# A 128-row bias matmul, and step B's loads issued by ScalarE

## The chip, the cores and the metric

The kernel runs on one core of a Trainium2 chip. The metric is the device time of one execution in microseconds (us). Three executions of the kernel before took 1357.65, 1356.60 and 1356.08 us; the median is 1356.6 us. Five engines work side by side, each through its own list of instructions in order: PE (matmuls; weight loads, PEld, are shown apart), DVE (VectorE), ACT (ScalarE), POOL (GpSimd) and SP (SyncE, which only issues DMAs here). Sixteen DMA engines move data for all of them.

## The reference

The input x has shape (4, 3008, 256): four batches. Cut to what matters:

```python
X = np.fft.rfft(x, axis=1)
Yr = Xr @ w_r - Xi @ w_i + b_r
Yi = Xr @ w_i + Xi @ w_r + b_i
Yr, Yi = shrink(Yr, 0.01), shrink(Yi, 0.01)     # sign(Y) * max(|Y| - 0.01, 0)
y = np.fft.irfft(Yr + 1j * Yi, n=3008, axis=1).reshape(12032, 256)
h = y @ moe_w_in                                # 256 -> 2048
g = np.maximum(h, 0) + moe_alpha * np.minimum(h, 0)
out = g @ moe_w_out                             # 2048 -> 256
```

All of it is float32.

## The kernel before, in words

A transform of length 3008 = 47 x 64 is done in two steps each way, as matmuls with tables: step A (length 47), step B (length 64), then the mixing step M with `w_r` and `w_i`, then steps C and D back. The two layers of the second part follow, tile by tile. The spectrum is worked on in 12 pairs of frequency slots (`NPAIR`), named q = 0 to 11.

The change lies in the first batch, b = 0, which runs alone at the start, while later batches are woven into the second part. Its steps B, M and C form a software pipeline: the loop `for t in range(NPAIR + 1)` near the end. In turn t, PE does in this order `b_mm(t)` (8 instructions of 128 columns into `ps_b`, L426), `m_mm(t - 1)` (first the bias matmul, L466, then 24 matmuls of 256 columns, L473, into `ps_m`) and `c_mm(t - 3)` (4 of 256 columns, L548, into `ps_c`). Between them stand the evictions: `b_evac` (ACT, L440) and `b_evac2` (DVE and POOL, L446 and L450), which split the result of step B into a rounded part `Xh` and a rest `Xl`; `m_evac` (ACT's `Yc`, L499, then DVE's `Y`, L500); `c_evac` (ACT's `zst`, L561, and the store of it to HBM, which ACT issues, L565). Every turn also runs a few operations of `pump`, which turns the weights of the second part into rounded part and rest (`conv`, L273 to L292, on ACT, DVE and POOL, from raw pieces `cw_s` that SP loads).

What step B reads was left in SBUF by step A (`a0_s`). `b_load(t + 3)` copies one pair of it into a tile `bt` by two DMAs of 128 KB, each from 4 partitions of 32 KB to 128 partitions of 1 KB. There are three such tiles, so the copy for pair t + 3 can start when `b_mm(t)` has read its own. For b = 0 POOL issues all of them: those of pairs 0 to 2 ahead of the loop, those of pairs 3 to 11 within it. For the later batches SP issues copies of the same shape from HBM.

The bias enters as a matmul of its own: `ones`, 4 rows x 128, is the stationary operand and `rows`, 4 rows x 512, the moving one (for b_r and b_i a rounded part and a rest each). It starts the accumulation of `ps_m`; the 24 products are added to it.

The order is written out by hand; each engine runs its own instructions in this order. DMAs that SP and ACT issue take one of eight completion semaphores in turn (`DMAHW0` to `DMAHW7` below), those of POOL one of eight others (`DMASW0` to `DMASW7`); an instruction that issues a DMA first waits until the DMA before it on the same semaphore has landed.

Of the kernel before, what the change touches and what calls it, by code (L numbers as in the profile page):

```python
# [10 lines left out]
F32R = mybir.dt.float32r  # L11
# [5 lines left out]
ALU = mybir.AluOpType  # L17
# [76 lines left out]
def fft_mix_moe(ctx, tc, x, w_r, w_i, b_r, b_i, w_in, w_out, alpha, la, rb, lc, rd, lf, cf, sel, out):  # L94
    nc = tc.nc
    B, S, C = x.shape
# [27 lines left out]
    const = ctx.enter_context(tc.tile_pool(name="const", bufs=1))  # L124
# [6 lines left out]
    V, G, A, PE = nc.vector, nc.gpsimd, nc.scalar, nc.tensor  # L131

    def f(t):
        return t.bitcast(F32)
# [32 lines left out]
    def half(h):  # L167
        t = const.tile([128, 2, FH * 2 * C], F32R, tag=f"half{h}", name=f"w{h}")
        wi_h[h] = t[:, 0].rearrange("p (w k f) -> p w k f", w=2, k=CT)
        wo_h[h] = t[:, 1].rearrange("p (m w f) -> p m w f", w=2, f=C)  # L170
# [5 lines left out]
    bias = [None]  # L176
# [6 lines left out]
    def first_bias():  # L183

        raw = work.tile([4, 2, C], F32, tag="Yt", name="bias_f", bufs=1)
        hi = work.tile([4, 2, C], F32R, tag="Yc", name="bias_h", bufs=1)
        pick = work.tile([4, 129], F32, tag="ot", name="sel", bufs=1)
        nc.gpsimd.dma_start(out=pick, in_=sel)
        for i, b in enumerate((b_r, b_i)):
            for k in range(2):  # L190
                nc.gpsimd.dma_start(out=raw[2 * i:2 * i + 2, k], in_=b.unsqueeze(0).to_broadcast([2, C]))
        rows = const.tile([4, 2, C], F32R, tag="bias", name="bias_p")
        ones = const.tile([4, 128], F32R, tag="wd", name="ones")
        bias[0] = ones, rows

        def parts():
            V.memset(lam_s, -LAM)
            V.tensor_copy(out=ones, in_=pick[:, 0:128])
            V.tensor_copy(out=hi, in_=raw)
            V.scalar_tensor_tensor(out=rows, in0=f(hi), scalar=pick[:, 128:129], in1=raw, op0=ALU.mult, op1=ALU.add)  # L200

        return parts

# [8 lines left out]
    def load_rb(n0, n1):  # L212
        nc.sync.dma_start(out=rb_s[:, n0:n1], in_=rb[:, n0:n1])

    def load_cf(n0, n1):
        nc.gpsimd.dma_start(out=cf_s[:, n0:n1], in_=cf[:, n0:n1])
# [93 lines left out]
    def pump(n):  # L310

        while n > 0:
            if not conv_ops:
                conv_fetch()
                second = conv_second(*conv_old.pop()) if conv_old else []
                first = conv_first(*conv_raw.pop(0)) if conv_raw else []
                first, second = ([(op,) for op in ops] for ops in (first, second))
                if first and second:
                    conv_ops.extend([second[0] + first[0], first[1], second[1], second[2] + second[3] + first[2]])
                else:  # L320
                    conv_ops.extend(first + second)
                if not conv_ops:
                    return
            for op in conv_ops.pop(0):
                op()
            n -= 1
# [12 lines left out]
    def a_load(b, g):  # L339

        if g == 0:
            ad[b] = dram.tile([NQ, R, C], F32, tag="ad", name=f"ad{b}")
        src = x[b].rearrange("(p r) c -> p r c", r=R)[:, 4 * g:4 * g + 4]
        if b == 0:
            ts = [x_s[:, 4 * g:4 * g + 4]]
        elif b == 1 and g in X1_TAGS:
            tags = X1_TAGS[g]
            ts = [work.tile([NP, 4 // len(tags), C], F32, tag=tag, name="xt", bufs={"Yl": None, "gh": 4}.get(tag, 1))
                  for tag in tags]
        else:  # L350
            ts = [work.tile([NP, 4, C], F32, tag="xt", name="xt")]
        if (b, g) == (0, 0):
            ts = [ts[0][:, 0:2], ts[0][:, 2:4]]
        n = 4 // len(ts)
        for i, t in enumerate(ts):

            for p in ((0, 80), (80, NP)):
                nc.sync.dma_start(out=t[slice(*p)], in_=src[slice(*p), n * i:n * i + n])
        xt[b, g] = ts
# [50 lines left out]
    def b_load(b, q):  # L410
        t = work.tile([128, 2, C], F32, tag="bt", name="bt", bufs=3)
        if b == 0:
            src = a0_s.rearrange("(w s q) g r c -> q w s (g r) c", w=4, s=2)[q]
        else:
            src = ad[b].rearrange("(w s q) r c -> q w s r c", w=4, s=2)[q]

        for k in range(2):
            (nc.gpsimd if b == 0 else nc.sync).dma_start(out=t[:, k], in_=src[:, k])
        bt[b, q] = t

    def b_mm(b, q):
# [560 lines left out]
    with tc.manual_schedule():  # L982
        nc.gpsimd.dma_start(out=lf_s, in_=lf)
        bias_parts = first_bias()
        nc.gpsimd.dma_start(out=la_s, in_=la)
        V.memset(idle, 0.0)
# [13 lines left out]
        for n, (b, g) in enumerate(seq):  # L1000
            a_mm(b, g)
            if n >= 1:
                a_evac(*seq[n - 1])
            if n == NG:
                for q in range(3):
                    b_load(0, q)
                split_mix()
                bias_parts()
# [6 lines left out]
        def run(fn, q, *args):  # L1015
            if 0 <= q < NPAIR:
                fn(0, q, *args)
# [9 lines left out]

        for t in range(NPAIR + 1):
            run(b_mm, t)
            run(b_load, t + 3)  # L1030
            run(c_evac, t - 4)
            run(b_evac, t)
            run(m_evac, t - 2)
            run(m_mm, t - 1, ps_h)
            run(b_evac2, t)
            run(c_mm, t - 3)
            if t < NPAIR:
                pump(PT[min(t, len(PT) - 1)])
            if t in (2, 5):
                load_rb(2 * t + 8, 2 * t + 14)  # L1040
            if t < 8 and t % 2 == 0:
                load_cf(3 * t, 3 * t + 6)
            if 5 <= t < 10:
                a_load(1, t - 3)
            if t == 10:
                half(1)
                conv_m[1] = FT
# [46 lines left out]
        for b in range(B):  # L1094
# [24 lines left out]
            for q in range(NPAIR if b + 1 < B else 0):  # L1119
                i = BO[b + 1] + BP * q  # L1120
                at(i - BL, b_load, b + 1, q)
                at(i, b_mm, b + 1, q)
                at(i, b_evac, b + 1, q)
                at(i, b_evac2, b + 1, q)
                at(i + MM, m_mm, b + 1, q)
                at(i + M2, m_mm2, b + 1, q, when=mid)
                for n, k in enumerate(MP):
                    at(i + k, m_part, b + 1, q, n, when=mid)
                at(i + MP[6], m_evac1, b + 1, q)
                at(i + CM, c_mm, b + 1, q)  # L1130
                at(i + CM, c_evac, b + 1, q)
# [60 lines left out]
        for k in range(len(spairs) + SLAG):  # L1192
# [9 lines left out]
            if k >= SLAG:  # L1202
                n, t = spairs[k - SLAG]
# [43 lines left out]
```

## Time and profile before

| | |
|---|---|
| median of three executions | 1356.6 us |
| profiled execution | 1356.09 us |
| its span, first to last instruction | 1354.3 us |
| PE busy | 1339.6 us (99%) |
| DVE busy | 1037.7 us (77%) |
| ACT busy | 759.2 us (56%) |
| POOL busy | 379.5 us (28%) |
| granted TensorE clock | full (2.4 GHz) in all 40 slices |

The rest of the 1356.09 us, 1.8 us, lies ahead of the first and behind the last instruction. The first batch's steps B, M and C take the stretch from about 31 to 91 us. POOL, with 28% over the whole span, is busy for 18.32 of the 20 us from 40 to 60 us, so that the shares of the whole span say little of this stretch. The DMA row of the page's slices shows 9 tenths in the first two slices, which reach to 68 us.

### The profile page before, as it was taken

How to read it: one execution, taken by the hardware profiler on the slowest of the kernel's cores; microseconds unless marked ns; L12 is line 12 of the kernel's file. 1: busy time of each engine (PE TensorE's matmuls, PEld its weight loads, DVE VectorE, ACT ScalarE, POOL GpSimd, SP SyncE). 2: the span in 40 equal slices, each digit the busy share in tenths (PEclk: the TensorE clock that was granted, in tenths of full speed). 3: DMA queues.
4: the chain of work that ended last, by engine and by line, in shares of the span. 5: the costliest groups of instructions: out<-in, count | busy, mean ns of one | idle time of the engine just before them, and what ended most of it. 6: DMA issues, size and time to landing. Idle time of an engine off the chain costs nothing.

```text
span 1354.3 us, 25104 instructions
## 1 busy us (share of the span) xinstructions
PE 1339.6 (99%) x9208; PEld 1252.3 (92%) x9208; DVE 1037.7 (77%) x1931; ACT 759.2 (56%) x1528; POOL 379.5 (28%) x403
## 2 busy tenths in 40 slices
PE   9999999999999999999999999999999999999998
PEld 5979989999999999999999999999999999999998
DVE  2766866777777777776768888888888888888885
ACT  3566645665566655545556555555565556555553
POOL 3854742221322232222212211122112111221222
PEclk9999999999999999999999999999999999999999
DMA  9964223342334312111110110111011101110001
GB/s 238 261 173 152 82 94 98 103 136 85 97 97 129 98 64 81 45 59 47 36 36 1 40 28 2 39 28 27 6 36 28 28 6 36 29 28 8 21 17 28
DMA packets 88119, 89.66 MB, mean 66 GB/s; under 512 B 42318, under 2 KB 70449, under 8 KB 87996
## 3 DMA queue, kind: packets, MB, share of 16 engines
q1 hardware_dynamic: 79428, 76.76, 19.9%
q0 software_dynamic: 5168, 8.02, 2.3%
q10 hardware_dynamic: 3399, 3.27, 0.8%
q8 instruction: 73, 1.20, 0.4%
q14 instruction: 51, 0.41, 0.1%
HBM read 50.49 MB, written 34.34 MB: 63 GB/s over the span
## 4 chain that ended last, share of the span: by engine, by line
PE 96%; DVE 1%; DMA 1%; issue 1%; ACT 1%; POOL 0%; ACTq 0%; DVEq 0%
PE ps_h L785 24%; PE ps_h L680 14%; PE ps_m L486 6%; PE ps_o L887 6%; PE ps_o L888 6%; PE ps_o L886 6%; PE ps_d L611 4%; PE ps_o L718 3%; PE ps_o L717 3%; PE ps_o L719 3%; PE ps_b L426 3%; PE ps_m L473 3%; PE ps_a L387 2%; PE o_last L719 2%; PE o_last L717 2%; PE o_last L718 2%
## 5 line engine op out<-in xcount | busy, mean ns | idle before, releaser
L785 PE MATMUL ps_h<-yh,w 128*128 128x512 f32 (+1 forms) x960 | 315.6, 390 | 0.0
L824 POOL TENSOR_TENSOR l<-t,h 128x512 fp32r<-128x512 f32 x98 | 127.0, 1296 | 496.6 <-ACT h L822 456.7
L785 PEld LDWEIGHTS ps_h<-yh,w 128*128 128x128 f32 x960 | 180.0, 188 | 33.2
L789 DVE SCALAR_TENSOR_TENSOR sq<-sq,beta_s,ps_h 128x512 f32<-128x512 f32 (+1 forms) x240 | 168.0, 733 | 55.0 <-ACT sq L788 54.2
L680 PE MATMUL ps_h<-yh,w 128*128 128x384 f32 (+1 forms) x704 | 206.2, 335 | 2.7 <-DVE q L687 2.7
L785 PE MATMUL ps_h<-yl,w 128*128 128x512 f32 (+1 forms) x480 | 186.3, 388 | 0.0
L691 ACT ACTIVATE gh<-q 128x384 fp32r<-128x384 f32 (+1 forms) x192 | 99.1, 516 | 148.6 <-DVE q L687 147.5
L687 DVE SCALAR_TENSOR_TENSOR q<-q,beta_s,ps_h 128x384 f32<-128x384 f32 (+1 forms) x192 | 115.5, 601 | 79.9 <-ACT q L686 78.1
L692 POOL TENSOR_TENSOR gl<-q,gh 128x384 fp32r<-128x384 f32 (+1 forms) x90 | 96.6, 1073 | 267.0 <-ACT gh L691 259.5
L804 ACT ACTIVATE dh<-sq 128x768 fp32r<-128x768 f32 x112 | 94.8, 846 | 118.0 <-DVE sq L789 72.8
L788 ACT ACTIVATE sq<-ps_h 128x512 f32<-128x512 f32 (+1 forms) x240 | 133.1, 586 | 27.5 <-PE ps_h L785 23.0
L680 PEld LDWEIGHTS ps_h<-yh,w 128*128 128x128 f32 x704 | 129.3, 189 | 5.7 <-DVE q L687 2.2
L822 ACT ACTIVATE h<-t 128x512 fp32r<-128x512 f32 x98 | 62.0, 633 | 104.5 <-DVE t L820 101.2
L680 PE MATMUL ps_h<-yl,w 128*128 128x384 f32 (+1 forms) x352 | 116.5, 331 | 0.0
L686 ACT ACTIVATE q<-ps_h 128x384 f32<-128x384 f32 (+1 forms) x192 | 91.4, 476 | 35.5 <-PE ps_h L680 34.2
L719 PE MATMUL ps_o<-w,gl 128*128 128x256 f32 x384 | 107.9, 281 | 1.7 <-POOL gl L692 1.7
L718 PE MATMUL ps_o<-w,gh 128*128 128x256 f32 x384 | 108.3, 282 | 0.0
L717 PE MATMUL ps_o<-w,gh 128*128 128x256 f32 x384 | 107.9, 281 | 0.0
L785 PEld LDWEIGHTS ps_h<-yl,w 128*128 128x128 f32 x480 | 90.5, 189 | 13.6
L819 DVE TENSOR_TENSOR dl<-sq,dh 128x768 fp32r<-128x768 f32 x98 | 93.4, 954 | 3.8 <-ACT dh L804 3.6
L888 PE MATMUL ps_o<-l,sw_a 128*128 128x256 f32 x294 | 82.0, 279 | 0.0
L886 PE MATMUL ps_o<-h,sw_a 128*128 128x256 f32 x294 | 81.9, 279 | 0.0
(211 smaller groups left out, 3625.6 us busy)
## 6 DMA issues: line engine op xcount, KB each, us to landing
zt<-zd SPq DMA_DIRECT2D x32, 384.0 KB
ad<-ast SPq DMA_DIRECT2D x48, 192.0 KB
bt<-ad SPq DMA_DIRECT2D x72, 128.0 KB
zd<-zst SPq DMA_DIRECT2D x36, 256.0 KB
xt<-in_x SPq DMA_DIRECT2D x21, 320.0 KB
out<-oT SPq DMA_DIRECT2D x152, 32.0 KB
cw_s<-in_moe_w_in SPq DMA_DIRECT2D x8, 512.0 KB
cw_s<-in_moe_w_out SPq DMA_DIRECT2D x8, 512.0 KB
```

The source lines that it names most:

```text
L680: PE.matmul(ps, wi_h[m // FH][:, w, ct, 128 * (m % FH):128 * (m % FH) + 128], a[:, ct, 0:n], start=(k == 0), stop=(k == 3 * CT - 1))
L687: V.scalar_tensor_tensor(out=q, in0=q, scalar=beta_s[:, m:m + 1], in1=ps, op0=ALU.mult, op1=ALU.add)
L691: A.activation(out=hi, in_=q, func=AF.Copy)
L717: PE.matmul(a, hi[:, t], w[:, 0], start=(i, k) in first, stop=False)
L718: PE.matmul(a, hi[:, t], w[:, 1], start=False, stop=False)
L719: PE.matmul(a, lo[:, t], w[:, 0], start=False, stop=(i, k) in last)
L785: PE.matmul(ps, wi_h[m // FH][:, w, ct, 128 * (m % FH):128 * (m % FH) + 128], a[:, ct, 0:w1], start=(k == 0), stop=(k == 3 * CT - 1))
L788: A.activation(out=q[:, j], in_=ps, func=AF.Relu, scale=-1.0)
L789: V.scalar_tensor_tensor(out=q[:, j], in0=q[:, j], scalar=beta_s[:, m:m + 1], in1=ps, op0=ALU.mult, op1=ALU.add)
L824: G.tensor_tensor(out=l24, in0=t24, in1=f(h24), op=ALU.subtract)
L886: PE.matmul(o, wh, gh, start=first, stop=False)
L888: PE.matmul(o, wh, gl, start=False, stop=last)
```

## The change

The tiles of the bias matmul become 128 rows high. DVE sets both to zero at the start, and the four rows are written into them as before. The loads of pairs 3 to 11 of the first batch are issued by ACT instead of POOL; those of pairs 0 to 2 stay with POOL. In the loop `b_load` is called behind `b_evac` instead of right behind `b_mm`. The later batches' loads stay on SP.

```diff
-        rows = const.tile([4, 2, C], F32R, tag="bias", name="bias_p")
-        ones = const.tile([4, 128], F32R, tag="wd", name="ones")
+        rows = const.tile([128, 2, C], F32R, tag="bias", name="bias_p")
+        ones = const.tile([128, 128], F32R, tag="wd", name="ones")
+        V.memset(f(rows), 0.0)
+        V.memset(f(ones), 0.0)
         bias[0] = ones, rows
 
         def parts():
             V.memset(lam_s, -LAM)
-            V.tensor_copy(out=ones, in_=pick[:, 0:128])
+            V.tensor_copy(out=ones[0:4], in_=pick[:, 0:128])
             V.tensor_copy(out=hi, in_=raw)
-            V.scalar_tensor_tensor(out=rows, in0=f(hi), scalar=pick[:, 128:129], in1=raw, op0=ALU.mult, op1=ALU.add)
+            V.scalar_tensor_tensor(out=rows[0:4], in0=f(hi), scalar=pick[:, 128:129], in1=raw, op0=ALU.mult, op1=ALU.add)
@@ b_load
         for k in range(2):
-            (nc.gpsimd if b == 0 else nc.sync).dma_start(out=t[:, k], in_=src[:, k])
+            (nc.sync if b else nc.gpsimd if q < 3 else nc.scalar).dma_start(out=t[:, k], in_=src[:, k])
@@ the loop over t
             run(b_mm, t)
-            run(b_load, t + 3)
             run(c_evac, t - 4)
             run(b_evac, t)
+            run(b_load, t + 3)
             run(m_evac, t - 2)
```

On ACT, in turn t = 6 of the loop, the kernel before has this order (each row is an instruction: its line, its kind, out<-in, and the semaphores it waits for):

```order
L561 ACTIVATE zst<-ps_c 128x512 [waits DMAHW5_49,PE_49]
L565 DMA zd_493<-zst 128x2x256 [waits Activation_49]
L440 ACTIVATE Xh<-ps_b 128x4x128 [waits PE_49,Pool_49]
L499 ACTIVATE Yc<-ps_m,lam_s 128x512 [waits DVE_49]
L273 ACTIVATE conv<-cw_s 128x512 [waits DMAHW6_49]
L282 ACTIVATE w_253<-conv 128x2x256 [waits DVE_49]
L283 ACTIVATE conv<-cw_s 128x512 [waits Pool_49]
```

and the changed kernel, in the same turn, this one (its line numbers are two higher):

```order
L563 ACTIVATE zst<-ps_c 128x512 [waits PE_49]
L567 DMA zd_495<-zst 128x2x256 [waits DMAHW7_49,Activation_49]
L442 ACTIVATE Xh<-ps_b 128x4x128 [waits PE_49,Pool_49]
L420 DMA bt<-a_83 128x1x256 [waits DMAHW4_49,DMAHW1_49]
L420 DMA bt<-a_83 128x1x256 [waits DMAHW3_49]
L501 ACTIVATE Yc<-ps_m,lam_s 128x512 [waits DVE_49]
L275 ACTIVATE conv<-cw_s 128x512 [waits DMAHW0_49]
L284 ACTIVATE w_255<-conv 128x2x256 [waits DVE_49]
L285 ACTIVATE conv<-cw_s 128x512 [waits Pool_49]
```

Two DMA issues, each with a wait of its own, now stand between `Xh` and `Yc`; all else keeps its place. On POOL the same turn reads, in the kernel before

```order
L418 DMA bt<-a_83 128x1x256 [waits DMASW5_49,DMASW6_49,DMASW4_49,PE_49]
L418 DMA bt<-a_83 128x1x256
L450 TENSOR_SCALAR Xh<-Xh 128x4x64 [waits Activation_49]
L450 TENSOR_SCALAR Xl<-Xl 128x4x64 [waits DVE_49]
L285 TENSOR_TENSOR conv<-conv 128x512 [waits DVE_49,Activation_49]
```

and in the changed kernel

```order
L452 TENSOR_SCALAR Xh<-Xh 128x4x64 [waits Activation_49]
L452 TENSOR_SCALAR Xl<-Xl 128x4x64 [waits DVE_49]
L287 TENSOR_TENSOR conv<-conv 128x512 [waits DVE_49,Activation_49]
```

Here the two issues, and their wait for PE, are gone. PE's own order is the same in both kernels.

## Rows read from the trace of the kernel before

**Rows 1.** The page's chain of waits, by engine, shares of the span

```profile
PE 96%; DVE 1%; DMA 1%; issue 1%; ACT 1%; POOL 0%; ACTq 0%; DVEq 0%
```

**Rows 2.** Chain of waits, 40 to 62 us (start us, us, what): one turn

```profile
44.93 0.89 PE ps_b L426 x8
45.83 0.43 PE ps_m L466
46.25 3.04 PE ps_m L473 x24
49.29 0.86 PE ps_c L548 x4
```

**Rows 3.** Timeline of PE, 45 to 47 us (start us, us, engine, line, op)

```profile
44.77 1.05 PE L426 MATMUL ps_b<-rb_s,bt 128*128 128x128 f32 x8
45.76 0.50 PE L466 MATMUL ps_m<-bias_p,ones 4*128 4x512 f32 x1
46.18 0.51 PE L473 MATMUL ps_m<-wr_s,Xh 128*128 128x256 f32 x2
...
46.65 0.40 PE L473 MATMUL ps_m<-wr_s,Xh 128*128 128x256 f32 x2
```

**Rows 4.** Groups, 31 to 92 us (busy us, mean ns | idle before <-releasers)

```profile
L473 PEld LDWEIGHTS ps_m<-wr_s,Xh 128*128 128x128 f32 x96 | 14.7, 189 | 3.0 <-issue 2.5 <-ACT conv L283 0.5
...
L466 PE MATMUL ps_m<-bias_p,ones 4*128 4x512 f32 x12 | 6.0, 497 | 0.0
```

**Rows 5.** Timeline of PE, 1000 to 1004 us: 512 columns on 128 rows

```profile
999.80 0.39 PE L785 MATMUL ps_h<-yh,w 128*128 128x512 f32 x1
1000.03 0.39 PE L785 MATMUL ps_h<-yl,w 128*128 128x512 f32 x1
```

**Rows 6.** Timeline of DVE, 0 to 9 us

```profile
7.29 0.69 DVE L402 COPY a<-ps_a 96x512 f32<-96x512 f32 x1 [6.35 <-PE ps_a L387]
```

**Rows 7.** Chain of waits, 74 to 92 us: the last pair's step B

```profile
81.53 0.89 PE ps_b L426 x8
```

**Rows 8.** Instructions on tile bt, 30 to 92 us (duration ns min/median/max, first and last start)

```profile
L418 POOL DMA_DIRECT2D bt<-a x18: 682/686/789, 30.9 to 68.2; - x18
...
DMA to landing us min/median/max: 4.9/7.3/10.3
```

**Rows 9.** Timeline of SP, 152 to 160 us

```profile
153.52 1.29 SPq L418 DMA_DIRECT2D bt<-ad  x2
```

**Rows 10.** Stretches: us, busy of PE, PEld, DVE, ACT, POOL, PEclk, DMA share, GB/s

```profile
20.00:24.00 4.00, 2.89 (x8) 0.86 (x7) 1.54 (x5) 2.50 (x5) 3.01 (x5) 1.00 1.05 369
31.00:78.00 47.00, 46.90 (x334) 42.47 (x334) 37.32 (x50) 25.75 (x46) 40.95 (x54) 1.00 1.00 247
158.00:161.00 3.00, 3.00 (x25) 3.00 (x24) 3.00 (x4) 1.38 (x3) 2.92 (x3) 1.00 0.28 90
```

**Rows 11.** DMA queues (packets, MB, share of 16 engines) and issues, 31 to 78 us

```profile
q1 hardware_dynamic: 5193, 5.90, 51.2%
q0 software_dynamic: 2971, 4.02, 36.5%
q10 hardware_dynamic: 1665, 1.61, 11.8%
...
xt<-in_x SPq DMA_DIRECT2D x2, 320.0 KB
xt<-in_x SPq DMA_DIRECT2D x4, 160.0 KB
```

**Rows 12.** Timeline of ACT, 50 to 62 us

```profile
56.53 0.60 ACT L440 ACTIVATE Xh<-ps_b 128x512 fp32r<-128x512 f32 x1 [0.50 <-PE ps_b L426]
...
59.66 0.63 ACT L282 ACTIVATE w<-conv 128x512 fp32r<-128x512 f32 x1 [1.39 <-DVE conv L288]
...
61.90 0.60 ACT L440 ACTIVATE Xh<-ps_b 128x512 fp32r<-128x512 f32 x1 [0.54 <-PE ps_b L426]
```

**Rows 13.** Who waited for whom, 31 to 91 us (us in total, times, longest)

```profile
ACT zst L561 <- PE ps_c L548: 10.1, 6, 2.5
```

## The prediction

> **What bounds the kernel now.** I read the page's chain of waits first: 96% of the span hangs on PE [rows 1], so what PE is spared counts, unless something else comes late in its place. The change touches one stretch, the first batch's loop over 12 pairs, so next I read the chain there. It runs through PE without a gap: 0.89 us of step B, 0.43 of the bias matmul, 3.04 of the 24 products, 0.86 of step C [rows 2], a turn of 5.22 us. The third view is the DMA: from 31 to 78 us its engines are counted as busy all the time (share 1.00), POOL for 40.95 of 47 us, ACT for 25.75 [rows 10]. A shorter turn on PE thus asks more of two resources that have little or nothing to spare.
>
> **The bias matmul.** The 4-row matmul starts at 45.76 and the next at 46.18, 0.42 us later [rows 3], for 512 columns. With 128 rows, 512 columns follow each other in 0.23 us (999.80 to 1000.03) [rows 5]. That is 0.19 to 0.20 us per pair for its own slot. Weight loads are caught as well: the one behind the bias matmul stands idle 3.0 us in all, 0.25 each in 12 pairs [rows 4], and the first two products take 0.51 us where two others take 0.40 [rows 3]: 0.11 us more, which I take to be that weight load, not hidden behind the 4-row matmul. Ahead of it the same seems to happen: eight matmuls of step B need 0.89 us in the chain [rows 2], 0.11 each, so the eighth starts at about 45.55, and the bias matmul follows 0.21 later instead of 0.11, another 0.10. Together 0.40 us per pair, 12 pairs [rows 4]: 4.8 us. Bounds: 12 x 0.20 = 2.4 us if only the slot shrinks, 4.9 us if all of it does; a loss is excluded, since the slot on 128 rows is in the trace. I take 4.8, because both weight-load terms are seen in the rows.
>
> The page TensorE: Matmul & The Clock Gate of the Trainium skill (section "Why this matters for your kernels") says that a single matmul on 32 rows takes the same time as one on 128; by it the saving would be nothing. The trace differs: 0.42 against 0.23 us.
>
> The two memsets stand at the start of DVE, which has 6.35 us of idle time there [rows 6]; I cost them at nothing. Were that cover gone, they would cost less than two of the 0.69 us copies next to them, 1.4 us.
>
> **The loads.** POOL loses 18 issues of 686 ns, 12.3 us [rows 8], and its wait for PE. ACT gains 18 issues. The nearest issue of that shape on a hardware queue is SP's copy for the later batches, 1.29 us for two [rows 9]. So ACT gets about 1.2 us per turn ahead of `Yc`, on top of 25.75 / 47 x 5.22 = 2.9 us of present work [rows 10], in a turn that PE would do in 4.82 us. `Yc` is needed only by DVE's `Y` and step C a turn later, and ACT waits 10.1 us for step C's matmuls in six of the turns [rows 13]. I let that slack hide the issues; a rival below takes it away.
>
> What isn't hidden so easily is who moves the data. From 158 to 161 us two copies of this shape from SP are under way; they move 90 GB/s at a DMA share of 0.28 of 16 engines [rows 10], that is on 4 to 5 engines and no faster for being two. I take it that a hardware queue puts these copies on the same four engines, each at about 22.5 GB/s, while POOL's go round. With all 16 busy, from 20 to 24 us, 369 GB/s give 23.1 GB/s for each [rows 10].
>
> The page DMA: Bandwidth & Descriptors of the Trainium skill (section "Why a DMA increments its semaphore by 16 and not by 1") has it so: the queues of SP and ACT use the lowest-numbered engines whose count divides both outer sizes, here 4 and 128, and GpSimd's queue moves on from one copy to the next. The share of 0.28 agrees; which engines they are no run here shows.
>
> So the four engines have this to do from 31 to 78 us: all queues moved 5.90 + 4.02 + 1.61 = 11.53 MB, 18 x 128 KB = 2.36 MB of it `bt` [rows 8, 11]. The other 9.17 MB spread over 16 engines are 0.573 MB for each; 2.36 MB on four are 0.590. Of the 1.163 MB, 0.082 are the loads of x for the second batch (2 x 320 KB and 4 x 160 KB [rows 11], over 16), which nobody needs before the loop ends. The eight semaphores of SP and ACT go round over both, so in the new order these loads wait for copies that ACT has issued. Time for it: the first of these loads is issued at 30.9 us [rows 8], the last pair's step B stands at 81.53 us [rows 7] and would come at 77.5 with ten pairs' saving of 0.40; with about 2.3 us for first packet and last landing (an estimate: the issue to landing is 4.9 us at the least [rows 8], about half of it transfer), 44.3 us are left.
> - At 23.1 to 24.5 GB/s (24.5 is what 98 GB/s on four engines would be, a tenth above the 90 of the row) and with x behind: 1.081 MB take 44.1 to 46.8 us. Late by 0 to 2.5 us.
> - With x in between: 1.163 MB, 47.5 to 50.3 us. Late by 3.2 to 6.0 us.
> - At the rates that the queues show now, in the crowded stretch (share x 16 x 47 us: 14.7 GB/s on q0, 15.3 on q1, 18.2 on q10 [rows 11]): 38 + 32 = 70 us. Late by 26 us.
>
> The last is the far end; I think it too high, because busy time in a crowd counts waiting. I take 1.5 us, in the middle of the first case, since the semaphores hold x back.
>
> **The sum.** 1356.09 us of the profiled execution - 4.8 + 1.5 = 1352.8. The median of the runs is 0.5 us above the profiled execution, so 1353.3 us. What follows the loop (step D, the second part) hangs on the loop's end and I let it shift as a whole.
>
> **Rivals.**
> 1. The four engines starve step B. The same copies at 20 GB/s instead of 23 take 1.081 / 20 = 54.1 us, 9.8 us late: -4.8 + 9.8 = 5.0 us slower, 1361.6 us. It decides from 22.0 GB/s downwards, where 1.081 MB take 44.3 + 4.8 us. For it: the share of 1.00 [rows 10] and 90 GB/s on four. Against it: 369 GB/s were moved with all engines busy, and SP's loads can slip. PE would then wait for `bt` before step B, late in the loop.
> 2. ACT becomes the bound. In the turn from 56.53 to 61.90 us it has 5.37 us from one `Xh` to the next, with a wait of 1.39 us for DVE, which itself stands behind `Y` and so behind `Yc` [rows 12]. With two issues of 1.2 us that turn becomes 6.6 us, 1.8 above 4.82. Two such turns unabsorbed cost 3.6 us: -4.8 + 1.5 + 3.6 = 0.3 us, 1356.9 us. A wait at the semaphores would come on top, since `Yc` and the conversions queue behind it. Against it: the slack of 10.1 us.
> 3. The change does not do what it says: the slow slot comes from going over from step B's operands to the bias's, not from the four rows. Then PE saves nothing, and the loads have 48 us, enough in the first case above: 1356.6 us. Against it: the late weight load behind the bias matmul, where the operands on both sides are of one kind.
>
> **Chances.** The forecast 0.47, with a range of its own from 1351.7 (nothing given back) to 1355. Rival 1: 0.25. Rival 2: 0.20. Rival 3: 0.08. The range that should hold 8 in 10 goes from 1351.3 to 1363: above it lies a part of rival 1 towards its 26 us. What can be told from no change is about 0.2%, 2.7 us: faster below 1353.9, slower above 1359.3. Of the forecast 0.39 of 0.47 falls below, of rival 2 0.04; of rival 1 0.19 falls above, of rival 2 0.03. So faster 0.43, same 0.35, slower 0.22.
>
> **What would show it.** Right: the bias matmul's next neighbour starts 0.23 us after it, the weight loads of the products lose their 3.0 us, a turn is near 4.8 us in the first half of the loop, and PE waits little for `bt`. Wrong: the slot stays at 0.42 us; or PE's wait for `bt` in the later turns adds up to over 4.8 us; or ACT's `zst` waits no more for PE, and PE waits for `Xh` or `Y` instead. The prediction fails as a whole if the loads land later than a turn allows from the first ones on.

## The result, and the profile after

The changed kernel takes 1365.43 us in the median (1364.06 to 1366.42, 5 runs) against 1356.6 us (1355.21 to 1357.65) for the kernel before: a ratio of 1.0063, 95% interval 1.0053 to 1.0074. It is 8.8 us slower where 3.3 us faster was forecast. The profiled execution took 1364.06 us, 7.97 us more than that of before.

The chain of waits of the changed kernel, by engine, has lost five points of PE, most of them to DMA and DVE [rows 1]:

```profile
PE 91%; DMA 4%; DVE 2%; ACT 1%; issue 1%; ACTq 0%; POOL 0%; SPq 0%; DVEq 0%
```

The same chain from 31 to 42 us (start us, us, what) shows an undisturbed turn near the loop's start. The bias matmul stands at 0.23 us and the 24 products at 2.84, where they had 0.43 and 3.04 [rows 2]: 0.40 us less in a pair. (Each piece of the chain is counted from the end of the one ahead of it.)

```profile
35.95 0.89 PE ps_b L428 x8
36.85 0.23 PE ps_m L468
37.08 2.84 PE ps_m L475 x24
```

Of the groups from 31 to 100 us, the weight load behind the bias matmul has 0.6 us of idle time left of 3.0, and the bias matmul itself now waits for DVE's `Y`, which it never did [rows 4]:

```profile
L475 PEld LDWEIGHTS ps_m<-wr_s,Xh 128*128 128x128 f32 x96 | 16.4, 198 | 0.6
...
L468 PE MATMUL ps_m<-bias_p,ones 128*128 128x512 f32 x12 | 6.1, 511 | 6.4 <-DVE Y L502 6.4
```

So the edit of the bias does what it was to do, and the loop is longer all the same. Where, the starts of the 12 bias matmuls tell (us, read from the traces; the experiments' rows are used below, and "freed semaphores" is the second run of that name, with the first `x` loads back on SP):

```
before            31.8 36.1 40.5 45.8 51.0 56.2 61.4 66.7 71.9 77.1 82.4 86.7
after             32.6 36.6 40.6 45.8 50.6 55.9 68.9 75.4 80.3 85.1 90.1 95.3
wide bias alone   33.2 37.6 41.6 46.4 51.2 56.0 60.9 65.9 70.7 75.6 80.5 85.9
" and zd on SP    32.5 36.8 40.8 45.6 50.4 55.3 60.1 65.1 70.0 74.8 79.6 83.5
freed semaphores  33.0 37.0 42.3 47.4 52.2 57.1 63.4 70.3 77.7 82.8 89.3 99.6
quarter on ACT    31.7 36.3 40.3 45.3 50.4 55.6 62.0 68.2 73.3 78.2 83.2 88.1
" behind Yc       32.0 36.0 40.0 44.8 49.6 54.5 59.3 64.3 70.6 75.7 80.6 85.7
```

From the first to the last they span 54.9 us before and 62.7 after. Eleven turns shorter by 0.40 would be 50.5, so 12.2 us were added: 8.2 in the turn from 55.9 to 68.9 (13.1 against 4.8), 1.7 in the next, some 2.3 in all others. Ahead of the loop and behind it the two differ by under 1 us.

ACT in that turn (timeline; in brackets the idle time before an instruction and what ended it): `zst` is done at 56.6, and its store is issued only at 62.87. Two loads of `bt` follow that take 2.94 us from the start of the first to the end of the second, which is held in its turn until 66.88, and `Yc`, for which DVE waits 8.7 us, comes at 67.47.

```profile
56.07 0.57 ACT L563 ACTIVATE zst<-ps_c 128x512 f32<-128x512 f32 x1
62.87 0.37 ACTq L567 DMA_DIRECT2D zd<-zst  x1
63.34 0.60 ACT L442 ACTIVATE Xh<-ps_b 128x512 fp32r<-128x512 f32 x1 [6.69 <-DMA bt<-a]
64.48 2.94 ACTq L420 DMA_DIRECT2D bt<-a  x2
67.47 0.69 ACT L501 ACTIVATE Yc<-ps_m,lam_s 128x512 f32<-128x512 f32 x1 [3.53 <-DMA xt<-in_x]
```

The store had to wait since the eight completion semaphores of SP's and ACT's queues go round over all their transfers in the order of the program. The eighth before this store was the second half of a `bt` load, issued at 47.02 and landed at 62.8, 15.8 us later. PE in the same stretch (timeline) wanted that very half, and then `Y`:

```profile
60.04 0.61 PE L428 MATMUL ps_b<-rb_s,bt 128*128 128x128 f32 x4
62.84 0.71 PE L428 MATMUL ps_b<-rb_s,bt 128*128 128x128 f32 x4 [2.19 <-DMA bt<-a]
68.94 0.79 PE L468 MATMUL ps_m<-bias_p,ones 128*128 128x512 f32 x1 [5.38 <-DVE Y L502]
```

That is 7.57 us of idle PE. It is paid a second time in the clock. In windows (us, busy of PE, PEld, DVE, ACT, POOL, PEclk, DMA share, GB/s) the granted clock falls to its lower level, 1.2 GHz, while PE stands idle, and it comes back at about 72.7, 3.8 us after PE has resumed:

```profile
66.00:68.00 2.00, 0.00 (x0) 0.00 (x0) 0.00 (x0) 0.53 (x1) 0.00 (x0) 0.50 0.26 89
70.00:72.00 2.00, 2.00 (x11) 2.00 (x11) 0.95 (x3) 1.68 (x3) 0.95 (x2) 0.50 0.12 40
72.00:74.00 2.00, 2.00 (x16) 1.97 (x15) 0.00 (x0) 0.96 (x2) 1.62 (x3) 0.84 0.69 122
74.00:76.00 2.00, 2.00 (x16) 1.88 (x15) 1.65 (x3) 1.43 (x3) 0.28 (x1) 1.00 1.03 375
```

Half of 3.8 us, 1.9, is what that costs by this count: about the 1.7 us that the next turn is too long.

From 31 to 78 us the DMA engines as a whole are less busy than before, a share of 0.68 against 1.00, and POOL 22.57 us against 40.95 [rows 10]:

```profile
31.00:78.00 47.00, 38.62 (x279) 36.67 (x280) 25.69 (x37) 19.89 (x35) 22.57 (x29) 0.93 0.68 205
```

Yet the loads land later. The 18 halves that ACT issues take 5.0 to 15.8 us from issue to landing, median 9.2, against 7.3 and at most 10.3 [rows 8]. How transfers end tells why (us, from the completion events; a transfer gives 16 signals, called parts here, and of ACT's halves only 4 wait for data):

```
kernel           transfer, issued by       issue   12th part  last part
wide bias alone  bt half, GpSimd           59.76     67.1       67.8
wide bias alone  zd store, ACT             62.22     71.6       72.0
after            weights, SP               50.48     54.6       58.0
after            zd store, ACT             52.30     57.4       64.5
half the pairs   bt half, GpSimd           58.89     61.7       68.1
half the pairs   zd store, ACT             55.19     59.9       70.9
```

In these rows of the changed kernel (and of one below in which ACT issues every second pair's loads) twelve parts land soon, and the last comes 3 to 11 us behind them, whichever queue the transfer went through. With all loads on GpSimd the sixteen end close together. Of all transfers with 16 such parts that were issued from 36 to 90 us, the 13th part is over 1 us behind the 12th in 16 of 24 in the changed kernel, but in 0 of 45 in the kernel before, 0 of 45 with the wide bias alone, and 0 of 57 in the run below with a quarter of the bytes on ACT. So there are four engines that are behind, and four is what ACT's copies use: in the window from 66 to 68 us above, where nearly all the packets are ACT's, the share of 0.26 is 4.2 engines of 16, and 89 GB/s are 22 for each of four. (The events do not say which engine a part is from; that it is the same four each time is the plain reading.)

### The profile page after: what moved, and what is told of

Its sections match the earlier page's. It is cut to its first block, busy times and chain, and to the rows that moved or that the text cites. A ratio compares the mean times of both kernels' runs of the same rounds, so it can differ in the third digit from the quotient of the medians.

```text
span 1362.3 us, 25093 instructions
## 1 busy us (share of the span) xinstructions
PE 1338.3 (98%) x9208; PEld 1253.0 (92%) x9208; DVE 1035.7 (76%) x1933; ACT 759.3 (56%) x1528; POOL 369.1 (27%) x385
## 4 chain that ended last, share of the span: by engine, by line
PE 91%; DMA 4%; DVE 2%; ACT 1%; issue 1%; ACTq 0%; POOL 0%; SPq 0%; DVEq 0%
PE ps_h L787 24%; PE ps_h L682 13%; PE ps_m L488 6%; PE ps_o L889 6%; PE ps_o L890 6%; PE ps_o L888 6%; PE ps_d L613 4%; PE ps_o L720 3%; PE ps_o L719 3%; PE ps_o L721 3%; PE ps_b L428 2%; DMA bt<-a 2%; PE ps_a L389 1%; PE o_last L721 1%; PE o_last L719 1%; PE o_last L720 1%
```

## The experiments

Two theories stood after the trace. T1: ACT's in-order queue, held by completion semaphores that come round too soon, keeps `Yc`, `Xh` and `zst` waiting. T2: four engines carry what sixteen did, and everything that has a part on them lands late, however it is issued. T3 is the price of the issues alone. All times are medians, ratios are to the kernel before.

**The bias alone.** The loads go back to GpSimd and to their old place:

```diff
-            (nc.sync if b else nc.gpsimd if q < 3 else nc.scalar).dma_start(out=t[:, k], in_=src[:, k])
+            (nc.gpsimd if b == 0 else nc.sync).dma_start(out=t[:, k], in_=src[:, k])
```

> The 128-row bias matmul alone, every load of step B issued by GpSimd at its old place. If the bias slot and the weight loads round it give back 0.40 us in each of 12 pairs, as both traces show it slot by slot, the time is 1356.6 - 4.8 = 1351.8 us (1350.8 to 1352.8). Rival: the loads' pace holds the pairs (DMA share 1.00 in that stretch of the kernel before), then TensorE's gain turns into a wait for `bt` and the time is 1355 to 1356.6.

1354.94 us, 0.9988 [0.9979, 0.9996]: 1.8 us of 4.8, between the two. TensorE has hardly a wait until 80 us, a turn is 4.85 us, and the loop is 2.2 us shorter in the profile (52.7), not 4.4; it also began 1.4 us later in that execution. The late turns lose it, the last alone 1.4 us (5.3 where 3.9 was due). ACT's timeline has one of the places, a `zd` store held until an `xt` load has landed:

```profile
75.97 0.58 ACT L563 ACTIVATE zst<-ps_c 128x512 f32<-128x512 f32 x1
78.13 0.37 ACTq L567 DMA_DIRECT2D zd<-zst  x1
78.59 0.60 ACT L442 ACTIVATE Xh<-ps_b 128x512 fp32r<-128x512 f32 x1 [2.04 <-DMA xt<-in_x]
```

**The loads alone.** The changed kernel with the 4-row bias of before.

> ScalarE issues the loads from the fourth pair on, at the changed kernel's place, and the bias matmul has its 4 rows. If the two edits simply add (the loads cost 13.4 us of waits, the bias gives 4.8), 1356.6 + 13.4 = 1370 us. If transfers set the pace of the pairs, TensorE's extra 0.40 us a pair lies in the waits and the time is that of the changed kernel, 1365 us; between the two, part of it.

1365.85 us, 1.0068 [1.0056, 1.0080]. The second forecast holds. Beside the late loads the bias is worth 0.4 us, which is within the intervals: the transfers set the pace, and what PE is spared turns into waiting.

**SyncE issues the loads.**

```diff
-            (nc.sync if b else nc.gpsimd if q < 3 else nc.scalar).dma_start(...)
+            (nc.gpsimd if b == 0 and q < 3 else nc.sync).dma_start(...)
```

> The same loads, the same two copies a pair and so the same four DMA engines, issued by SyncE instead of ScalarE; 128-row bias. Theory T1 (ScalarE, held at an issue, keeps `Yc`, `Xh` and `zst` waiting behind it): most of the 13.4 us of waits go, 1352 to 1357 us, and ScalarE has no wait over 3 us before `Yc` or `Xh`. Theory T2 (the copies land 10 to 14 us after they were issued, since four engines carry them, whoever issues): the waits stay, now before `ps_b` for `bt`, 1361 us or more; SyncE's own loads queue behind them. Theory T3 (ScalarE's 0.55 us per issue): 1352 us.

1366.86 us, 1.0078 [1.0066, 1.0090]: as T2 says in time, but not in the place. ACT is free of issues and still waits, for weights that SP issues in between and that now come late (waits from 31 to 100 us: us in total, times, longest):

```profile
ACT conv L275 <- DMA cw_s<-in_moe_w_in: 9.3, 2, 7.3
...
PE ps_m L468 <- DVE Y L502: 8.1, 7, 2.0
...
ACT conv L275 <- DMA cw_s<-in_moe_w_out: 6.7, 2, 5.5
```

The halves land 4.3 to 11.4 us after their issue. This run takes the issues off ACT without parting the theories, since SP's queue is in order too. It does show that the loss doesn't need ACT as the issuer.

**The stores off ACT.**

```diff
-            nc.scalar.dma_start(out=dst, in_=st)
+            nc.gpsimd.dma_start(out=dst, in_=st)
```

> The changed kernel, with the 12 stores of step C's results of the first batch (`zd`) issued by GpSimd instead of ScalarE. T1 in the form that a store, held by its completion semaphore, stops ScalarE (the 6.7 us before `Xh` at 63 us): 1357 to 1361 us. T1 by the loads' own semaphores, or T2: 1363 to 1367 us, with the waits behind the `bt` issues.

1367.28 us, 1.0085 [1.0070, 1.0100]. The hold only moves on to the next instruction of ACT that needs a semaphore, a load, with `Yc` behind it (ACT's timeline; some of the time may be GpSimd's, since the same move beside the wide bias alone costs 2.8 us, 1357.72 against 1354.94 below):

```profile
56.33 0.59 ACT L442 ACTIVATE Xh<-ps_b 128x512 fp32r<-128x512 f32 x1
62.69 1.16 ACTq L420 DMA_DIRECT2D bt<-a  x2
63.90 0.69 ACT L501 ACTIVATE Yc<-ps_m,lam_s 128x512 f32<-128x512 f32 x1 [6.98 <-DMA bt<-a]
```

**Half the pairs on ACT** (pairs 4, 6, 8, 10; the others on GpSimd).

> The changed kernel, but ScalarE issues only the loads of pairs 4, 6, 8 and 10; GpSimd those of the others. T2: the four engines get less than half of the extra load, landing falls below the lead of about two turns and most of the 13.4 us goes: 1353 to 1359 us. If each ScalarE-issued pair costs a wait of its own (a share of 4/9): 1358 to 1361 us.

1360.00 us, 1.0019 [1.0010, 1.0028]: about half the loss (5.1 of 10.5 us over the bias alone) for 8 of the 18 copies; it lies in the second forecast and 1.0 us above the first, too near to part them. Its trace gave the rows on the late four parts above.

**Sixteen engines, by SyncE.** Each half is cut by source row into four copies:

```diff
+            for k in range(2):
+                for w in range(4):
+                    nc.sync.dma_start(out=t[32 * w:32 * w + 32, k], in_=a0_s[24 * w + 12 * k + q:24 * w + 12 * k + q + 1].rearrange("p g r c -> p (g r) c"))
```

> SyncE issues the loads from the fourth pair on, as in the run where SyncE issued two copies a pair (1366.9 us), but each copy is cut into four by its source row: 8 copies of 32 KB a pair, each from one row of 32 pieces, so that each lands with 16 increments instead of 4. Same bytes, same 1 KB pieces; four times as many issues, and four times as many completion semaphores taken. T2 (four engines carry what sixteen could): loads land in 4 to 8 us instead of 9 to 15, SyncE's other loads no longer end with four late engines, and the time is 1352 to 1359 us. T1 (semaphores held and in-order issue are the cost): no better than 1367 us, or worse, since 8 copies hold all 8 semaphores.

1377.58 us, 1.0158 [1.0139, 1.0178]. T2's landings came true, 2.7 to 5.7 us, all 16 parts within some 2 us of each other; its time did not: that is the one that T1 named, 1367 us or worse. But it needs no semaphore to explain it. SP issues 72 copies of 0.59 us (group of that line from 31 to 100 us: ns min/median/max), 4.7 us of a turn, and the weights stand behind them (waits from 31 to 115 us):

```profile
L422 SPq DMA_DIRECT2D bt<-a x72: 502/589/1842, 32.3 to 95.8; - x72
ACT conv L275 <- DMA cw_s<-in_moe_w_in: 20.0, 4, 9.9
ACT conv L275 <- DMA cw_s<-in_moe_w_out: 16.7, 3, 9.3
```

**Half the bytes on SyncE**, once as four copies on 16 engines, once as one on four; GpSimd has the other half.

> 128-row bias. From the fourth pair on, GpSimd issues one half (128 KB) of each load and SyncE the other half, cut into four copies of one source row each, which land with 16 increments; `zd` stays on ScalarE. To be read against the next run, which differs only in that SyncE's half is one copy that lands with 4 increments. T2 (crowding of four engines): no landing ends with four late engines, copies land in 3 to 6 us, and this run is the faster of the two by 3 us or more: 1351 to 1356 us against 1358 to 1363. T1 (semaphores alone): four times as many copies hold four times as many semaphores, and this run is the slower one.

> As the run before, with SyncE's half of each load as one copy of four source rows (four engines). T2: half of the extra load on the four engines, as in the run where ScalarE took four of nine pairs (1360.0 us): 1358 to 1363 us, landings of 128 KB in 8 to 14 us. T1: faster than the run before, 1352 to 1356 us.

1362.29 us (1.0041 [1.0027, 1.0055]) and 1359.76 us (1.0027 [1.0017, 1.0038]). The order is T1's, though the intervals overlap; the second's time is T2's, and neither theory has both times. In the second SP's halves landed 4.6 to 12.2 us after issue, and four late parts show in 17 of 38 transfers; the first, with `zd` on SP as well,

> The first run of this call with `zd` stores issued by SyncE too, so that ScalarE issues nothing in the pairs. If a held store on ScalarE is what is left: 1350.5 to 1353 us, under the first. If SyncE's row of issues (4 copies, 1 store, weights and `xt` a pair) is too long: 1355 us or more.

took 1360.89 us, 1.0032 [1.0019, 1.0045], and there too ACT waited 12.2 + 9.1 us for weights behind SP's issues. On SP the theories can't be parted: by these waits its own issues hold the kernel up before the relief of the engines can show.

**The same issues, a quarter of the bytes.** ACT's 18 issues stay, with their semaphores in the same order, but each carries one source row of four; GpSimd issues the other three.

```diff
+                nc.scalar.dma_start(out=t[0:32, k], in_=a0_s[12 * k + q:12 * k + q + 1].rearrange("p g r c -> p (g r) c"))
+                nc.gpsimd.dma_start(out=t[32:128, k], in_=src[1:4, k])
```

> The changed kernel with the same 18 issues on ScalarE at the same places and with the same completion semaphores in the same order, but each ScalarE copy carries one source row of four (32 KB, landing with 16 increments); GpSimd issues the other three rows of each half (96 KB). T1 or T3 (the issues on ScalarE and the semaphores they take and wait for are the cost in themselves): 1361 to 1366 us, with ScalarE held for 5 us or more at one issue. T2 (holds are long only because 128 KB on four engines lands 9 to 16 us after its issue): landings of 3 to 8 us, no ScalarE wait over 3 us, 1353 to 1357 us.

1359.36 us, 1.0018 [1.0006, 1.0030]: 6.1 us of the changed kernel's 10.5 over the bias alone are gone. ACT's copies land in 3.2 to 9.0 us, the 6.7 us hold is gone, and the DMA share is back at 0.92. T1 and T3 had said 1361 to 1366, T2 1353 to 1357, so the time lies between; of T2's signs the landings came nearly (3 to 8 us was said). What is left seems to be ACT's waiting for its own issues ahead of `Yc` (waits of ACT, 31 to 93 us):

```profile
ACT Yc L505 <- issue: 5.9, 4, 2.7
ACT Yc L505 <- DVE conv L277: 2.3, 1, 2.3
```

**The same with the load's call behind the one for `Yc`.**

> The run in which ScalarE issues one row of four (1359.4 us), with the load's call moved behind the one that puts `Yc` on ScalarE. There ScalarE spent 1.2 to 2.7 us a turn on two issues with `Yc` behind them. If what was left over the kernel with the wide bias alone (4.4 us) is `Yc` kept waiting by issues: 1354.5 to 1357 us. If it is the loads' lateness: 1359 us or more.

1358.19 us, 1.0007 [0.9996, 1.0017]. The loop of the profile shrinks from 56.4 to 53.7 us; the medians differ by 1.2 us and their intervals overlap, and the profiled execution was the fastest of 12, 3.3 us below the median. The median lies between the two forecasts. That `Yc` behind the issues is the rest is likely, and not shown.

**Freed semaphores.** `zd` and the second batch's `x` loads on GpSimd, so that a load of ACT waits for a transfer three turns old.

> The changed kernel (loads from the fourth pair on by ScalarE, 128 KB on four engines each) with the `zd` stores and the second batch's `x` loads issued by GpSimd, so that a load of ScalarE waits for a transfer three turns old instead of about one and a third. T1 (semaphores taken again too soon hold ScalarE): landings still 8 to 15 us, but the 7 us holds go and the time is 1353 to 1358 us. T2 alone (the loads are too late for TensorE, however they are issued): 1361 us or more, with TensorE waiting at `ps_b` for `bt`.

1378.62 us, 1.0155 [1.0133, 1.0176]; the pairs began at 41.4 us, since the first `x` loads kept GpSimd. With these back on SP:

> As the run with freed semaphores, but the second batch's first two `x` loads stay on SyncE, since on GpSimd they put the start of the pairs off by 9 us (first bias matmul at 41.4 us). T1: ScalarE's loads wait for transfers that are three turns old and are hardly held; 1353 to 1358 us, the pairs from first to last bias matmul in 53 to 56 us. T2: landings of 9 to 17 us as in that run, and the pairs need 62 to 67 us as there; 1363 to 1368 us.

1367.26 us, 1.0073 [1.0058, 1.0089], the loop 66.6 us long. These are T2's numbers, but in part by luck. The last two turns alone take 16.9 us (82.7 to 99.6) against 10.2 in the changed kernel, and there PE waits for GpSimd, which now issues the stores and most `x` loads too and is busy for 17.73 of 18 us (the window in the columns of above, then PE's waits from 31 to 105 us):

```profile
82.00:100.00 18.00, 13.15 (x74) 11.85 (x74) 13.13 (x20) 7.81 (x14) 17.73 (x26) 0.81 0.61 191
...
PE ps_m L475 <- POOL Xh L452: 4.9, 2, 3.7
PE ps_b L428 <- DMA bt<-a: 3.4, 3, 2.0
```

So the time of this run doesn't part the theories; the turns ahead of that stretch can. From the first to the tenth bias matmul it is 42.4 us with the wide bias alone, 52.5 in the changed kernel, 49.7 here and 46.5 with a quarter on ACT (one execution each). Of 10.1 us lost there, freed semaphores give back 2.8, and three quarters of the bytes taken off the four engines 6.0.

The loads stay late here. Landings take 5.4 to 17.7 us; after one at 53.0 eleven more land up to 87.8 us, that is a pair in 6.3 us (34.8 / 11 x 2), where a turn of PE is 4.85. And a hold comes back without any semaphore to wait for. The second of two issues lasts 3.90 and 4.99 us, each time with five earlier halves on their way (ACT's timeline of the later one), and `Yc` is behind it:

```profile
70.22 0.54 ACTq L420 DMA_DIRECT2D bt<-a  x1
...
70.80 4.99 ACTq L420 DMA_DIRECT2D bt<-a  x1
75.83 0.69 ACT L501 ACTIVATE Yc<-ps_m,lam_s 128x512 f32<-128x512 f32 x1 [4.69 <-issue]
```

**The bias with the stores elsewhere**, since a held `zd` store ate some of its gain.

> The 128-row bias with all loads of step B on GpSimd (1354.9 us), and the first batch's 12 stores of `zd` issued by GpSimd too. In that run ScalarE waited 2.0 us before `Xh` behind a store held until an `xt` load had landed. Theory: this hold on ScalarE ate part of the bias's 4.8 us; then 1351 to 1353.5 us. Rival: GpSimd (busy 0.94 of 44 to 56 us there) becomes the bound with 12 issues of 0.7 us more: 1355 to 1359 us.

> As the run before, but SyncE issues the `zd` stores, which leaves GpSimd as it was. Theory (a held store on ScalarE ate the gain): 1351 to 1353.5 us. Rival: SyncE, waiting for `zst` in order, starts its weight and `xt` loads later: 1355 us or more.

> The kernel before (4-row bias, loads on GpSimd) with only the first batch's `zd` stores moved to SyncE. With the 128-row bias the same move gave 1354.1 us. If the move itself brings nothing while TensorE is never idle in the pairs: 1356 to 1357 us, and the bias is worth 2 to 3 us on top of it; if it brings the gain alone: 1354 to 1355 us.

On GpSimd 1357.72 us (1.0008 [0.9999, 1.0017]), the rival's time. POOL is busy 42.74 of 47 us from 31 to 78, but PE waits for it only 0.8 us there, so that POOL is the bound is likely and not shown. On SyncE 1354.14 us (0.9979 [0.9970, 0.9989]), between the two forecasts, the fastest version here and better than both kernels, with a loop of 51.0 us, 3.9 below that of before, in a profiled execution that was the fastest of 9 and 1.4 us below the median. The move alone, with 4 bias rows, gives 1356.30 us (0.9994 [0.9983, 1.0006]), nothing that can be told. So the wide bias is worth 2.2 us on that ground, by intervals that overlap at their ends; against the bias alone on ACT's stores the 0.8 us gained are within the intervals.

## Why the prediction was wrong

**What bounds the kernel.** Read rightly: PE's chain in the loop, with DMA and POOL near their limit.

**The bias.** The size of the step holds to the hundredth: in the chain, slot 0.43 to 0.23, products 3.04 to 2.84, 0.40 us a pair. So does the reading of the idle weight load. The shares of its three terms do not hold, and that they add up right is luck in part. By the starts of the matmuls, as the prediction read them, the stretch ahead of the bias matmul shrinks from 0.98 to 0.81 us (0.10 was forecast), its own slot from 0.43 to 0.32 (0.20; the sign of being right, a neighbour 0.23 us later, didn't come in starts), and the products from 2.96 to 2.84 (0.11). What failed is to book 12 x 0.40 in full as time. It was worth 1.8 us alone, 2.2 with the stores moved, and 0.4, within the intervals, beside the late loads. Rival 3 falls, since the slot shrank between the same neighbours.

The Trainium skill's rule that a single matmul on 32 rows costs what one on 128 does (TensorE: Matmul & The Clock Gate, "Why this matters for your kernels") does not agree with this trace, where it is 4 rows: 0.43 against 0.23 us in the chain, 0.32 by starts. No run here has 32 rows.

**The memsets.** Right: 0.48 and 0.17 us, with 5.30 us idle behind them (DVE's timeline):

```profile
0.92 0.48 DVE L194 MEMSET bias_p<- 128x512 f32 x1 [0.92 <-PEq L1229]
1.38 0.17 DVE L195 MEMSET ones<- 128x128 f32 x1
...
6.92 0.69 DVE L404 COPY a<-ps_a 96x512 f32<-96x512 f32 x1 [5.30 <-PE ps_a L389]
```

**ACT's issues.** Mostly 0.54 to 0.62 us each, 1.15 for two, as taken from SP's row (1.2); four of the 18 took 1.0 to 1.6. Their slack was taken for cover of the issue time alone. The hold at a semaphore, which rival 2 names and does not price, is the larger part: ACT is idle for 6.69 and 3.53 us in one turn, of which the two issues themselves are 1.1. The prediction's own sign of being wrong is what came: `zst` waits 0.5 us for PE instead of 10.1, and PE waits for `Y`, 6.4 us, and 2.8 for `bt`, 0.6 of it ahead of the loop (waits, 31 to 100 us):

```profile
PE ps_m L468 <- DVE Y L502: 6.4, 3, 5.4
...
PE ps_b L428 <- DMA bt<-a: 2.8, 2, 2.2
```

**The loads: the step that failed.** "Late by 0 to 2.5 us", of which 1.5 was taken, rests on four engines at 23.1 to 24.5 GB/s and on "x behind". The four engines were right, the rate and the order were not. Its own row of 158 to 161 us gives 22.5 GB/s for each of four, and its range began above that. From 31 to 68 us the changed kernel's queues moved this (DMA view of that stretch):

```profile
DMA packets 6722, 7.71 MB, mean 208 GB/s; under 512 B 2572, under 2 KB 4872, under 8 KB 6718
```

Twelve halves of `bt` had landed by 68.3, 1.57 MB; a sixteenth of the other 6.14 MB and a quarter of these make 0.777 MB on each of the four, 21.0 GB/s (an estimate: it takes the rest as spread evenly). And the `x` loads did not stay behind: four of the six pieces were issued between 52.9 and 72.8 us, before the last `bt` at 77.37. They are three quarters of the 0.082 MB, so the prediction's own sum is 1.081 + 0.062 = 1.143 MB; at 21.0 GB/s it takes 54.4 us, 10.1 late. With 1.9 for the clock, which the prediction put at nothing without a reason, -4.8 + 10.1 + 1.9 = 7.2 us stand against the 7.97 measured. So the term that was taken as 1.5 us came out as some 10: the case with x in between, at a rate just below the 22.0 from which rival 1 decides. That the new sum comes so near is luck in part. The last half lands at 88.0 us, where the sum has it at 30.9 + 2.3 + 54.4 = 87.6; but the four engines were not busy throughout (all engines have a share of 0.12 from 70 to 72 us, while ACT was behind with its issues), and PE did not wait for that half: it lost its time in the middle of the loop.

Rival 1 had the cause and the side. Its 1361.6 us has 20 GB/s where 21.0 came out, and leaves out the `x` loads (2.9 us at 21.0) and the clock. It had the place only in part: not `bt` late in the loop, but an in-order queue in its middle.

The rule that the queues of SP and ACT use the lowest-numbered engines, the largest number up to 16 that divides both outer sizes (the Trainium skill, DMA: Bandwidth & Descriptors, "Why a DMA increments its semaphore by 16 and not by 1"), is borne out further than before: one-row copies of 32 pieces land with 16 increments, and the four late parts show in all queues' transfers. Which numbers the engines have no run shows.

**The cause, as far as shown.** With the issues and semaphores kept and three quarters of the bytes taken off the four engines, 6.1 of 10.5 us go, and the four late parts go with them (0 of 57 transfers); with the bytes kept and the semaphores freed, the first nine turns get back 2.8 of 10.1 us, and the loads stay as late. With the bytes kept and SP as the issuer nothing comes back. So the lateness of four engines is the root, and the hold on ACT is how it reached PE here: taken away in one place, it came back at the next load, at SP's weights, or in the issue itself. Open are the 4.4 us that ACT's issues cost even with a quarter of the bytes, of which 1.2 may be `Yc`'s place in the order.

## What to carry to other kernels

Before a transfer is moved to another queue, count the bytes for each DMA engine by the copy's outer size, over everything that has a part there: a share of all engines far below 1 says nothing when four of them are full. Then follow who waits for the slowest part: with completion semaphores taken in turn, one late transfer holds an unrelated instruction of an in-order engine, and all that is queued behind it. A gain on the bounding engine is worth its full size only as far as the next resource leaves room, so test it alone first.

## What was not expected of the hardware

- Issues on ACT's queue are not always 0.54 us. With five halves of 128 KB still on their way, the next lasted 3.90 and 4.99 us in the run with freed semaphores; the ends, 68.78 and 75.79, come 0.4 and 1.7 us after an earlier half had landed.
- Engines that are behind for one queue are behind for all: the last four parts of GpSimd's transfers came up to 7.3 us after the other twelve (half the bytes on SP as one copy), those of SP's up to 8.4 (SP issues the loads), those of ACT's own stores up to 11.
- Cutting a copy of four source rows into one-row copies brought the landing from 4.3 to 11.4 us (SP as the issuer) down to 2.7 to 5.7, but each costs SP 0.59 us of issue, and with 72 of them the weights behind them came late: 1377.58 against 1366.86 us.
- An idle stretch of 5.38 us behind another of 2.19 cost PE 1.9 us more at the lower clock.
